# One level of Strassen for the third batch's second feed-forward product, on one Trainium2 core

## The chip, the core and the metric

The kernel runs on one core of a Trainium2 chip. The metric is the device time of one execution in microseconds (us). TensorE is PE below, VectorE DVE, ScalarE ACT, GpSimd POOL, and SyncE, which issues most of the transfers, SP. Every engine works through its own queue in order and waits on semaphores for the others.

## What is computed

For four batches of 768 rows, a retention layer (8 heads of 64) is followed by a Fourier mixing block and a feed-forward pair. The recurrence over time is done in chunks of 128 rows in the kernel; only the second half matters for this change:

```python
# attn_out: (4, 8, 768, 64) -> x: (4, 768, 512)
X = np.fft.fft(np.fft.fft(x, axis=1), axis=2)
u = x + np.real(X)
un = (u - mean(u)) / np.sqrt(var(u) + 1e-06)
ch = np.maximum(un @ w_ch1, 0.0) @ w_ch2     # 512 -> 2048 -> 512
out = u + ch
```

Inputs and output are float32; the matmuls run on float16 with float32 sums.

## The kernel before, in words

The four batches are pipelined: while the feed-forward of batch b runs, the attention of batch b + 1 is computed beside it (casts on POOL, transposes as transfers on SP, mask products and chunk states on DVE, scaled outputs on ACT), then its mixing. Each piece of work is a unit with a due time in units of batches; `emit` (L1387) sorts all units by it, and the tile framework arranges the instructions of each engine in a fixed queue. `held` (L150) ties a unit's instructions to the order in which they were written; units that are not held may be moved by the framework's scheduler.

The mixing of a row block kb (128 rows) is `s2_unit` (L993): four small matmuls into `pq`, two ACT copies, two DVE steps into u (L1019, L1022), two POOL additions. `norm_unit` (L1046) follows: statistics on DVE, then the normalised block on ACT; `unT_unit` (L1071) transposes it, for batches 2 and 3 by a transfer.

The feed-forward of batches 1 and 2 goes in two row tiles of 384. `h_unit` (L1087) computes 128 hidden features: four matmuls of 384 columns, then a ReLU on ACT or DVE by the list ACT_ROWS (L62) into ht16. `ch_unit` (L1124) computes the second product of a 128-row block: 16 matmuls of 512 columns into one PSUM tile, one DVE instruction that scales and adds u (L1135), and one transfer out.

The last batch does the second product by one level of Strassen, in Winograd's form, for three groups of 256 rows. The hidden features are split into two halves and the output columns into two halves, so that rows, features and columns make two-by-two blocks. `hp_unit` (L1169) computes hidden features n and n + 8 for 256 rows (eight matmuls of 256 columns) and does their ReLUs on ACT, the last one half on DVE. `hidden_sums` (L1193) forms four sums of hidden blocks on DVE, at the points that SUMS (L59) lists. `wsum_unit` (L1156) forms four sums of blocks of w_ch2 on DVE, in eight instructions, into buffers of the load pool `inp`. `p_unit` (L1205) computes one of the seven products: eight matmuls of 256 columns, then DVE instructions (L1235) that scale the PSUM tile and add it to u or to the output tile. Products 1, 6 and 7 accumulate in one PSUM tile which DVE reads after each of them. The order is 1, 4, 5, 6, 2, 7, 3. The PSUM pool `ps_pm` has three tiles, shared by the first and the second product.

Loads of q, k and v (`load_unit`, L189) go through the pool `inp` of 11 buffers, 12 loads to a batch, issued in SP's queue among the transposes and the outputs. Due times: TS1 and LD1 for attention and loads, DM1 and LAST_MIX for the mixing of row blocks 3 to 5, WS for the weight sums.

Of the kernel before, what the change touches and what calls it, by code (L numbers as in the profile page):

```python
# [12 lines left out]
ALU = mybir.AluOpType  # L13
f32 = mybir.dt.float32
f16 = mybir.dt.float16
# [50 lines left out]
def kernel(  # L66
# [17 lines left out]
    inp = pool("inp", 11)  # L84
# [100 lines left out]
    in_of, a_of = {}, {}  # L185
    w_dma = []
    srcs = {"q": q, "k": k, "v": v}

    def load_unit(b, i, after=None, names="qkv"):  # L189
        def run():  # L190
            h0 = 2 * PAIR_ORDER[i]
            for name in names:
# [3 lines left out]
                t = inp.tile([P, 2, NCH, D], f32, tag="in32", name=f"{name}32")  # L196
# [17 lines left out]
    def first_load(name, i, eng):  # L214
        def run():
            h0 = 2 * ORD0[i]
            t = in_of[name, 0, i] = inp.tile([P, 2, NCH, D], f32, tag="in32", name=f"{name}32")
# [869 lines left out]
    def h_unit(b, rt, fb):  # L1087
        def run():
# [6 lines left out]
            if fb in ACT_ROWS[rt]:  # L1095
# [46 lines left out]

    def flat(t):
        return t.rearrange("p h c d -> p (h c d)").bitcast(f16)

    def spare(n, name):
        return flat(inp.tile([P, 2, NCH, D], f32, tag="in32", name=name))[:, 0:n]
# [3 lines left out]
    sg = htf[:, 8 * DM:12 * DM].rearrange("p (s n k) -> p s n k", s=2, n=8)  # L1151

# [3 lines left out]
    def wsum_unit(k, part):  # L1156


        def run():
            n0, n1 = 4 * part, 4 * part + 4  # L1160
            t = seven["t", k, part] = spare(4 * 256, "wsum").rearrange("p (n m) -> p n m", n=4)
            a, b = {1: ((0, 1), (0, 0)), 2: ((1, 1), None), 3: ((1, 1), (0, 1)),
                    4: ((1, 0), None)}[k]
            in1 = half_of(w216, *b, n0, n1) if b else seven["t", k // 2, part]
            nc.vector.tensor_tensor(out=t, in0=half_of(w216, *a, n0, n1), in1=in1,
# [3 lines left out]
    def hp_unit(b, g, n):  # L1169

        def run():
            unT = lb[b]["unT"]
            if (g, n) == (0, 0):
                seven["s4"] = spare(8 * P, "s4").rearrange("p (n k) -> p n k", n=8)
# [18 lines left out]
    def hidden_sums(g, n, which):  # L1193

        sl = slice(max((0,) + tuple(m + 1 for m in SUMS[g == 2] if m < n)), n + 1)
        a11, a12 = hg[:, sl, 0, 0:P], hg[:, sl, 1, 0:P]
        a21, a22 = hg[:, sl, 0, P:256], hg[:, sl, 1, P:256]
        s1, s2, s4 = sg[:, 0, sl], sg[:, 1, sl], seven["s4"][:, sl]
        ops = ((s1, a21, a22, ALU.add), (s2, s1, a11, ALU.subtract),
# [5 lines left out]
    def p_unit(b, g, k):  # L1205


        def run():
# [6 lines left out]
            if k in (1, 2, 4):  # L1215
                seven[name] = ps_pm.tile([P, 2, 256], f32, tag="pm", name="ps7")
# [272 lines left out]
```

## Time and profile before

| | us |
|---|---|
| median of 3 runs | 241.77 (240.67 to 242.31) |
| the profiled execution | 240.73 |
| its span, first to last instruction | 238.7 |
| PE busy in the span | 225.4 |
| DVE busy | 187.4 |
| ACT busy | 125.3 |
| POOL busy | 81.4 |

The granted TensorE clock is full throughout. In the rows of a profile, "x" is the number of instructions, shapes are partitions by elements, "out<-in" are the program's names, and L is the line in the kernel. A timeline row has the start, the time from the first start to the last end of instructions merged into it, and in brackets how long the engine had been idle before it and what ended that. Busy time includes overlap of neighbours of under 0.1 us. In the chain of waits each row is a start, a length and the work that held up the rest.

### The profile page before, as it was taken

What the parts mean: (1) busy time and instruction counts of PE and PEld (TensorE: products, weight loads), DVE (VectorE), ACT (ScalarE), POOL (GpSimd) and SP (SyncE); (2) the same over time, 40 slices, a digit from 0 to 9 for tenths busy, and PEclk for the clock granted to TensorE, in tenths of its full rate; (3) what the DMA queues carried; (4) which work ended last, traced back from release to release, by engine and by line L of the source; (5) the groups of instructions that cost most, each with busy time, mean ns of one, the idle gap of its engine ahead of it and who ended that gap; (6) DMA issues with size and microseconds to landing.
All of it is one profiled execution on the core that took longest, in us unless ns stands there. A gap on an engine that the chain in (4) does not pass through costs nothing.

```text
span 238.7 us, 5575 instructions
## 1 busy us (share of the span) xinstructions
PE 225.4 (94%) x2135; PEld 155.3 (65%) x2135; DVE 187.4 (79%) x460; ACT 125.3 (52%) x273; POOL 81.4 (34%) x148
## 2 busy tenths in 40 slices
PE   0788999999999999999999999999999999999993
PEld 0356779756775646765567446655666468888893
DVE  8789887958898889986886829977895885867473
ACT  5989759674865444840247415822257326072430
POOL 8378802665300097850000826940002410220000
PEclk9999999999999999999999999999999999999999
DMA  7999999999999489979999577696100261031202
GB/s 179 233 270 239 237 206 207 210 251 248 241 235 208 72 191 221 203 138 132 249 279 218 116 161 203 130 138 156 53 3 0 45 154 25 3 110 23 91 0 91
DMA packets 100954, 36.80 MB, mean 154 GB/s; under 512 B 91456, under 2 KB 97984, under 8 KB 100928
## 3 DMA queue, kind: packets, MB, share of 16 engines
q1 hardware_dynamic: 96704, 32.25, 64.2%
q0 software_dynamic: 4224, 4.19, 10.6%
q8 instruction: 17, 0.28, 0.5%
q14 instruction: 9, 0.07, 0.1%
HBM read 27.26 MB, written 6.29 MB: 141 GB/s over the span
## 4 chain that ended last, share of the span: by engine, by line
PE 82%; DVE 6%; DMA 5%; ACT 2%; issue 1%; POOL 1%; SPq 0%; DVEq 0%; ACTq 0%
PE psc L1131 23%; PE psh L1092 21%; PE psh L1179 9%; PE ps L1231 5%; PE psh L1109 3%; PE wkA L667 3%; DMA qTz<-q16z 3%; PE ps L850 3%; DMA k<-in_k_dram 2%; PE wkY L721 2%; PE pq L1012 2%; PE ps L830 1%; DVE atm L539 1%; PE wkY L717 1%; PE wkK L686 1%
## 5 line engine op out<-in xcount | busy, mean ns | idle before, releaser
L1131 PE MATMUL psc<-w,ht 128*128 128x512 f16 x288 | 67.7, 379 | 0.0
L1092 PE MATMUL psh<-unT,w 128*128 128x384 f16 x320 | 59.5, 326 | 0.0
L1040 POOL TENSOR_TENSOR u<-u,x 128x256 f32<-128x256 f32 x21 | 13.3, 635 | 117.1 <-DVE u L1019 104.8
L1131 PEld LDWEIGHTS <-ht 128*128 128x128 f16 x288 | 27.3, 98 | 26.5
L1092 PEld LDWEIGHTS <-w 128*128 128x128 f16 x320 | 29.9, 98 | 15.9 <-DMA unT<-un 0.4
L1096 ACT ACTIVATE ht<-psh 128x384 f16<-128x384 f32 x46 | 22.3, 489 | 23.7 <-PE psh L1092 23.2
L670 DVE TENSOR_TENSOR atm<-wkA,maskp 128x512 f16<-128x512 f32 x36 | 23.6, 680 | 1.7 <-PE wkA L667 1.7
L1184 ACT ACTIVATE ht<-psh 128x512 f16<-128x512 f32 (+1 forms) x24 | 13.7, 571 | 15.6 <-PE psh L1179 11.0
L1179 PE MATMUL psh<-unT,w 128*128 128x256 f16 x192 | 21.6, 273 | 0.0
L1098 DVE TENSOR_SCALAR ht<-psh 128x384 f16<-128x384 f32 x34 | 18.7, 549 | 2.7 <-PE psh L1092 2.5
L1056 ACT ACTIVATE un<-u,stats 128x512 f16<-128x512 f32 x21 | 14.8, 717 | 10.7 <-DVE stats L1052 7.6
L1179 PEld LDWEIGHTS <-w 128*128 128x128 f16 x192 | 18.7, 98 | 2.1
L1135 DVE SCALAR_TENSOR_TENSOR ob<-psc,stats,u 128x512 f32<-128x512 f32 x18 | 13.4, 743 | 8.5 <-PE psc L1131 8.3
L696 DVE SCALAR_TENSOR_TENSOR s<-s,gk,wkK 128x128 f16<-128x128 f16 x48 | 16.1, 336 | 2.4 <-ACT s L692 1.6
L729 ACT ACTIVATE x<-wkY,gexp 128x384 f16<-128x384 f32 x24 | 12.9, 580 | 9.0 <-PE wkY L721 8.9
L1051 DVE BATCH_NORM_STATS2 bst<-u 128x6 f32<-128x512 f32 x21 | 14.4, 686 | 4.0 <-POOL u L1042 3.8
L1231 PEld LDWEIGHTS <-ht 128*128 128x128 f16 x152 | 14.1, 98 | 2.3 <-issue 0.6
L441 POOL TENSOR_SCALAR kd<-k,gexp 128x384 f16<-128x384 f32 x24 | 13.8, 585 | 3.3 <-DMA k<-in_k_dram 3.3
L667 PE MATMUL wkA<-qTz,kT 128*128 128x256 f16 x72 | 13.2, 273 | 0.3 <-DMA qTz<-q16z 0.3
L1042 POOL TENSOR_TENSOR u<-u,x 128x256 f32<-128x256 f32 x21 | 13.3, 635 | 0.0
L1014 ACT COPY qn<-pq 128x128 f32<-128x128 f32 x18 | 4.9, 274 | 15.0 <-PE pq L1012 15.0
L1203 DVE TENSOR_TENSOR ht<-ht 128x512 f16<-128x512 f16 (+2 forms) x21 | 8.1, 385 | 5.9 <-ACT ht L1184 5.6
(194 smaller groups left out, 400.9 us busy)
## 6 DMA issues: line engine op xcount, KB each, us to landing
q<-in_q_dram SPq DMA_DIRECT2D x16, 384.0 KB, 6.0
k<-in_k_dram SPq DMA_DIRECT2D x16, 384.0 KB, 5.6
v<-in_v_dram SPq DMA_DIRECT2D x16, 384.0 KB, 5.7
out_dram<-ob SPq DMA_DIRECT2D x23, 256.0 KB, 2.4
w<-in_moe_w_ch_dram POOLq DMA_DIRECT2D x8, 512.0 KB, 10.9
unT<-un SPq DMA_TRANSPOSE x15, 2.5
kT<-kd SPq DMA_TRANSPOSE x10, 3.0
qTz<-q16z SPq DMA_TRANSPOSE x8, 3.8
```

The costliest lines, as they stand in the source:

```text
L441: kc = nc.gpsimd.tensor_scalar(out=kd[:, :, h2, :], in0=k32[:, h2], scalar1=gkd[:, h0 + h2:h0 + h2 + 1], scalar2=1.0, op0=ALU.mult, op1=AL ...
L667: mm = nc.tensor.matmul(wk[:, c2], st["kT"][:, c, :], st["qT"][:, :, c, :], start=True, stop=True)
L670: nc.vector.tensor_tensor(out=st["atm"][:, 2 * part:2 * part + 2], in0=wk, in1=maskp[:, PAIR_ORDER[i]].unsqueeze(1).to_broadcast([P, 2, 2, ...
L696: nc.vector.scalar_tensor_tensor(out=s16[:, c], in0=s16[:, c - 1], scalar=gk2[:, hp:hp + 1], in1=wk[:, c - c0], op0=ALU.mult, op1=ALU.add)
L1051: nc.vector.bn_stats(bst, u[:, kb, :])
L1056: nc.scalar.activation(un, u[:, kb, :], AF.Identity, bias=stats[:, kb, 0:1], scale=-1.0)
L1092: nc.tensor.matmul(psh, w116[:, cb, fb * P:(fb + 1) * P], unT[:, cb, rt * 384:(rt + 1) * 384], start=(cb == 0), stop=(cb == 3))
L1096: nc.scalar.activation(ht16[:, fb, :], psh, AF.Relu, bias=0.0, scale=-1.0)
L1098: nc.vector.tensor_scalar(out=ht16[:, fb, :], in0=psh, scalar1=-1.0, scalar2=0.0, op0=ALU.mult, op1=ALU.max)
L1131: nc.tensor.matmul(psc, ht16[:, fb, rb3 * P:(rb3 + 1) * P], w216[:, fb, :], start=(fb == 0), stop=(fb == NFB - 1))
L1179: nc.tensor.matmul(psh[:, t], w116[:, cb, fb * P:(fb + 1) * P], unT[:, cb, g * 256:(g + 1) * 256], start=(cb == 0), stop=(cb == 3))
L1231: nc.tensor.matmul(dst, lhsT, rhs[:, c0:c1], start=bool(new and n == 0), stop=(n == 7), skip_group_check=True)
```

## The change

Batch 2, the third, takes the same form as batch 3: three groups of `hp_unit`, the seven products, and no `ch_unit`. In numbers, 128 first-product matmuls of 384 columns and 96 second-product matmuls of 512 become 192 and 168 matmuls of 256. Its units are not held; those of batch 3 are. Further:

- The weight sums are made once, due at 1.65 to 1.95 instead of 2.88 to 2.98, so beside the second batch. They stay until the end: three of the four in `wide`, four load buffers taken out of the pool (11 becomes 7), one in cd16 and sd16, tables that are no longer needed then. Until then loads use `wide` in their turn; the last batch's loads use the seven buffers alone.
- In the second batch (b = 1) all ReLUs but those of every fourth feature block go to ACT; before, ACT had 8 of 16 and 10 of 16.
- The hidden sums become three in the first half of the features and two at the end of the second, then one over all features after product 2, in place in a block that product 2 has read, and a last one after product 1. The order of the products becomes 2, 1, 4, 6, 5, 7, 3 in both batches; the scheduler is free to move those of batch 2. Product 4 shares a PSUM tile with 2 (it gets the other half), and 5 with 3. DVE adds 4 to u and to the output tile in two instructions of 256, 5 by itself.
- Due times: attention beside the third batch is stretched (TS7, 0.69 instead of 0.585), the mixing of its row blocks 3 to 5 has times of its own (MIX7), and loads are due one by one (LD1, LD2).

The core of the diff:

```diff
-LD0, LD1 = (0.223, 0.312), (-0.370, 0.140)
+TS7 = (-0.040, -0.020, 0.048, 0.69)
+LD0, LD1, LD2 = (0.223, 0.312), (-0.2425, -0.115, 0.0125, 0.14), (-0.2425, -0.115, 0.0125, 0.25)
-WS = (-0.12, -0.02)
+WS = (-0.35, -0.05)
-SUMS = ((3, 7), (2, 5, 7))
+MIX7 = {3: (0.01, 0.08, 0.10, 0.20), 4: (0.30, 0.38, 0.40, 0.45), 5: (0.42, 0.50, 0.52, 0.57)}
+SEVEN = 2
...
-    inp = pool("inp", 11)
+    inp = pool("inp", 7)
...
+    wide = const.tile([P, 4, 2, NCH, D], f32, tag="wide")
+    loads = [0]
+
+    def in_tile(name, b):
+        n = loads[0] % 11
+        loads[0] += 1
+        if b < B - 1 and n >= 7:
+            return wide[:, n - 7]
+        return inp.tile([P, 2, NCH, D], f32, tag="in32", name=f"{name}32")
...
-            if fb in ACT_ROWS[rt]:
+            if fb in ACT_ROWS[rt] or b + 1 == SEVEN and fb % 4:
...
+    def t_of(k, part):
+        if k == 1:
+            return (cd16, sd16)[part].rearrange("p a b -> p (a b)").rearrange(
+                "p (n m) -> p n m", n=4)
+        return tw[:, k - 2, 4 * part:4 * part + 4]
...
-            if n in SUMS[g == 2]:
-                hidden_sums(g, n, (0, 1) if n == 7 else (0, 1, 2, 3))
+            if n == 3:
+                hidden_sums(0, 4, (1, 2, 3))
+            elif n == 7:
+                hidden_sums(4, 8, (1, 2))
...
+        ops = {1: (s1, a21, a22, ALU.add), 2: (s2, s1, a11, ALU.subtract),
+               3: (a21, a11, a21, ALU.subtract), 4: (a12, a12, s2, ALU.subtract)}
...
-            name, half = {1: ("a", 0), 6: ("a", 0), 7: ("a", 0), 2: ("b", 0), 4: ("dc", 0),
-                          5: ("dc", 1), 3: ("dc", 1)}[k]
+            name, half, new = {2: ("bd", 0, 1), 1: ("a", 0, 1), 4: ("bd", 1, 0), 6: ("a", 0, 0),
+                               5: ("c", 0, 1), 7: ("a", 0, 0), 3: ("c", 0, 0)}[k]
...
-            if k == 1:
+            if k == 2:
+                hidden_sums(0, 8, (4,))
+            elif k == 1:
                 add(left, ps, ri, left)
-                hidden_sums(g, 7, (2, 3))
-            elif k == 2:
+                hidden_sums(4, 8, (3,))
+            elif k == 4:
                 ob = seven["ob"] = obp.tile([P, DM], f32, tag="ob", name="ob")
-                add(ob[:, 0:256], ps, ri, left)
+                add(ob[:, 0:256], seven["bd"][:, 0], ri, left)
+                add(u[:, j, 0:256], ps, rj, u[:, j, 0:256])
...
-        if b == B - 1:
+        if b >= SEVEN:
+            pinned = held if b == B - 1 else lambda unit: unit
             for g in range(3):
-                majors += [held(hp_unit(b, g, n)) for n in range(8)]
-                majors.append(held(rstd_unit(b, g, 2)))
-                majors += [held(p_unit(b, g, k)) for k in (1, 4, 5, 6, 2, 7, 3)]
+                majors += [pinned(hp_unit(b, g, n)) for n in range(8)]
+                majors.append(pinned(rstd_unit(b, g, 2)))
+                majors += [pinned(p_unit(b, g, k)) for k in (2, 1, 4, 6, 5, 7, 3)]
```

More of the change, by code (lines that the diff above doesn't have):

```diff
@@ L1251, in run @@
                 add(right, ps, ri, right)
-            elif k == 5 and tail:
-                flat_dc = seven["dc"].rearrange("p t m -> p (t m)")
-                add(u[:, j, 0:384], flat_dc[:, 0:384], rj, u[:, j, 0:384])
-                add(u[:, j, 384:DM], seven["e"], rj, u[:, j, 384:DM])
             elif k == 5:
-                add(pair(u[:, j]), seven["dc"], rj, pair(u[:, j]))
+                for dst, c0, c1 in outs:
+                    uj = u[:, j, 256 + c0:256 + c1]
+                    add(uj, dst, rj, uj)
             elif k == 7:
```

72 lines of the change are left out of this document (34 added, 38 removed).

## The prediction

> **What bounds the kernel now.** I read the busy shares first, then the busy time by stage, then the chain of work that ended last, then the timelines of PE and DVE where products are evicted.
>
> ```profile
> PE 225.4 (94%) x2135; PEld 155.3 (65%) x2135; DVE 187.4 (79%) x460; ACT 125.3 (52%) x273; POOL 81.4 (34%) x148
> ```
> ```profile
> core 0: us, PE busy (x) PEld busy (x) DVE busy (x) ACT busy (x) POOL busy (x), PEclk, DMA share, GB/s
> 142.40:168.00 25.60, 25.60 (x226) 16.05 (x226) 22.24 (x52) 11.17 (x28) 12.31 (x21) 1.00 0.74 157
> 168.00:194.40 26.40, 26.40 (x196) 15.94 (x195) 22.17 (x51) 11.23 (x25) 3.64 (x6) 1.00 0.19 43
> ```
>
> The two windows are the third batch (b = 2). PE is busy for all 52.0 us of it, so PE sets its length. But DVE is busy for 44.4 us, 85%: only 7.6 us of cover are left there. ACT has 29.6 us free.
>
> ```profile
> 170.06 0.22 PE wkA L667 x2
> 170.28 0.65 PE psh L1092 x4
> 170.93 0.29 PE wkY L717 x10
> 171.22 0.42 PE wkY L721 x12
> 171.64 5.94 PE psh L1092 x36
> ...
> 183.80 10.36 PE psc L1131 x48
> 194.16 0.23 PE pq L1012 x4
> 194.40 7.00 PE psh L1179 x64
> ...
> 215.53 6.23 PE ps L1231 x56
> ```
>
> These rows of the chain price PE's work: 0.165 us for a 384-column matmul of the first product, 0.216 for a 512-column one of the second, 0.109 for the paired first product, 0.111 for a 256-column matmul of the seven products (0.89 for a product of eight). Note that the 48 matmuls at 183.80 ran without any gap: each block has its own PSUM tile and needs DVE once in 3.5 us. The seven products are different. Products 1, 6 and 7 gather in one tile, so 6 cannot start before DVE has read 1, nor 7 before DVE has read 1+6. The last batch shows what that costs:
>
> ```profile
> 206.40 1.03 PE L1231 MATMUL ps<-wsum,ht 128*128 128x256 f16 x8 [0.42 <-DVE u L1235]
> ```
> ```profile
> 201.84 0.43 DVE L1187 TENSOR_SCALAR ht<-psh 128x256 f16<-128x256 f32 x1 [1.60 <-ACT ht L1184]
> 202.29 0.89 DVE L1203 TENSOR_TENSOR ht<-ht 128x512 f16<-128x512 f16 x2
> 203.10 0.16 DVE L1068 RECIPROCAL stats<-stats 128x2 f32<-128x2 f32 x1
> 203.36 0.48 DVE L1235 SCALAR_TENSOR_TENSOR u<-ps,stats,u 128x256 f32<-128x256 f32 x1
> 203.76 0.41 DVE L1203 TENSOR_TENSOR s<-ht 128x512 f16<-128x512 f16 x1
> 204.10 0.42 DVE L1203 TENSOR_TENSOR ht<-ht 128x512 f16<-128x512 f16 x1
> 204.43 0.74 DVE L1235 SCALAR_TENSOR_TENSOR u<-ps,stats,u 128x512 f32<-128x512 f32 x1
> 205.09 0.47 DVE L1019 SCALAR_TENSOR_TENSOR u<-pq,g,qn 128x256 f32<-128x256 f32 x1
> 205.48 0.47 DVE L1022 SCALAR_TENSOR_TENSOR u<-pq,g,qn 128x256 f32<-128x256 f32 x1
> 205.88 0.47 DVE L1235 SCALAR_TENSOR_TENSOR u<-ps,stats,u 128x256 f32<-128x256 f32 x1
> ```
>
> Product 6's eviction starts at 205.88 and ends at 206.35; product 7 starts on PE at 206.40. Ahead of it stood only sums, four evictions and two mixing steps: in the last batch DVE has little else to do. In the third it also carries the attention of the last batch.
>
> For the prices of that other work, from start to start where instructions follow without a gap:
>
> ```profile
> 151.12 0.68 DVE L1051 BATCH_NORM_STATS2 bst<-u 128x6 f32<-128x512 f32 x1
> 151.72 0.67 DVE L670 TENSOR_TENSOR atm<-wkA,maskp 128x512 f16<-128x512 f32 x1
> 152.31 0.17 DVE L1052 BATCH_NORM_AGGREGATE stats<-bst 128x2 f32<-128x6 f32 x1
> 152.40 0.66 DVE L1051 BATCH_NORM_STATS2 bst<-u 128x6 f32<-128x512 f32 x1
> 152.98 0.33 DVE L696 SCALAR_TENSOR_TENSOR s<-s,gk,wkK 128x128 f16<-128x128 f16 x1
> 153.22 0.17 DVE L1052 BATCH_NORM_AGGREGATE stats<-bst 128x2 f32<-128x6 f32 x1
> ...
> 172.33 0.56 DVE L1098 TENSOR_SCALAR ht<-psh 128x384 f16<-128x384 f32 x1 [0.69 <-PE psh L1092]
> 172.81 1.01 DVE L746 TENSOR_TENSOR xab<-x 128x768 f16<-128x768 f16 x2
> 173.74 0.55 DVE L1098 TENSOR_SCALAR ht<-psh 128x384 f16<-128x384 f32 x1
> ...
> 189.68 0.69 DVE L1165 TENSOR_TENSOR wsum<-w,wsum 128x1024 f16<-128x1024 f16 x1
> ```
>
> So: statistics 0.60, aggregate 0.09, mask product 0.59, state step 0.24, a 384-wide ReLU 0.48, two folds 0.93. From the fence above: half a mixing step 0.39, a 256-wide eviction 0.40, a 512-wide one 0.66, a 512-element hidden sum 0.34 to 0.46 (the latter if it waits for the one before it; 0.40 taken where either may be). Instructions start some 0.07 us before the one ahead ends, so the half ReLU (0.43 long) counts 0.36 and a 1024-element sum (0.69) 0.62.
>
> **The change, part by part.**
>
> *PE in the third batch.* 96 second-product matmuls (96 x 0.216 = 20.7) become 168 of 256 columns (168 x 0.111 = 18.7); the first product goes from 128 x 0.165 = 21.1 to 192 x 0.109 = 21.0. All else on PE stays. Gain 2.1 us (1.9 to 2.3), and only if PE is never kept waiting.
>
> *DVE in the third batch.* Out go 14 ReLUs (0.48 each), 6 wide evictions (0.66) and the 8 weight sums (0.62): 15.7 us. In come, for each of three row pairs, six 512-element sums, one of 1024, half a ReLU, six 256-wide evictions and one of 512: 6 x 0.40 + 0.62 + 0.36 + 6 x 0.40 + 0.66 = 6.4, or 19.3 us. Net +3.6 us: 44.4 + 3.6 = 48.0 of the 49.9 that PE would need. 96% on average, with work that comes in bursts, means stalls; the order in which the changed program's instructions stand in DVE's queue says where.
>
> The windows show PE at 100% of this stage and DVE at 85%. The Trainium skill (Perfetto Trace Analysis, Identifying the Most-Contended Engine) says to find the engine with the highest occupancy and to relieve that one first. By that rule the relief of PE counts whole and the result would be the first rival's below; the windows agree that PE is the fullest, but by the sum above the fullest engine changes with the edit.
>
> *Third pair of rows (the last products of the batch).* Let X be the end of the pair's first product. On DVE, in order, up to product 6's eviction: mixing block 0 (0.79), half ReLU (0.36), half of block 1 (0.39), sum (0.40), other half (0.39), sum (0.40), statistics 0 (0.60), the 1024 sum (0.62), aggregate (0.09), eviction 1 (0.40), sum (0.35), mixing block 2 (0.79), two statistics (1.20), aggregate, an eviction of 4, aggregate, the other of 4 (0.09 + 0.40 + 0.09 + 0.40), eviction 6 to its end (0.47): 8.2 us. PE would be ready for product 7 at X + 0.23 + 2 x 0.89 + 0.23 + 3 x 0.89 = 4.9. PE waits 3.3 us, 3.8 if the statistics of block 2 also wait for POOL, whose two additions to it (0.64 us each by the row below) start only behind that block's mixing. I take 3.6; the low end, 2.5, is for a queue that starts a little ahead.
>
> ```profile
> 185.04 0.64 POOL L1040 TENSOR_TENSOR u<-u,x 128x256 f32<-128x256 f32 x1 [1.19 <-DVE u L1019]
> ```
>
> Before, these mixing steps and statistics lay under 10.4 us of gap-free second product; that cover is gone. The last batch's first product stands behind product 3 on PE, and the transpose of block 1, whose normalising waits for the same aggregate, comes in at about the same time.
>
> *Second pair.* From its X, DVE has up to eviction 6: statistics, aggregate, four state steps, half ReLU, two sums, two folds, the 1024 sum, two folds, eviction 1, a sum, two mask products, two evictions, eviction 6: 0.60 + 0.09 + 0.96 + 0.36 + 0.80 + 0.93 + 0.62 + 0.93 + 0.40 + 0.35 + 1.18 + 0.80 + 0.47 = 8.5. PE reaches product 7 after outputs, products 2 and 1, masks, 4, masks, 5 and 6, outputs, and the next pair's first ReLU tile: 0.71 + 1.78 + 0.22 + 0.89 + 0.44 + 1.78 + 0.43 + 1.0 = 7.25. That is 1.25 us; the next pair's third ReLU tile then waits for product 3's tile, which DVE reads behind two folds, up to 0.9 more. I take 2.0 (1.2 to 2.4).
>
> *First pair.* DVE has room; product 6 waits for eviction 1 by 0.25 to 1.1, the upper end if the normalising that stands between this pair's ReLUs on ACT holds them. I take 0.7.
>
> *Last batch.* Its products now go 2, 1, 4, 6, 5, 7, 3 and its fourth sum is one 1024-element step ahead of eviction 1, which slips from 203.36 to about 204.05; then a sum, two evictions instead of one wide, the mixing: eviction 6 ends at 206.85 instead of 206.35, +0.5. In the other two pairs eviction 1 ends 3.3 us behind the first product and product 6 is ready at 2.7: +0.6 to 0.7 each, where before there was no wait. Sum 0.4 (sums at their shortest) to 1.9; I take 1.5.
>
> *Second batch and loads.* 9 ReLUs (9 x 0.48) move from DVE to ACT, which the page shows half idle, and 8 weight sums (8 x 0.62) come onto DVE: 0.7 us net there, beside gap-free matmuls. I count 0 (-0.2 to +0.5). Loads of the last batch have 7 buffers instead of 11: the last head pair's loads wait for the first pair's casts, and its own casts stand on POOL behind a mixing step that DVE reaches some 8 us after the first X. The mask products that need them stand on PE some 20 us after it (the rest of the products, the next first product, two products more). Casts, of the length of POOL's 0.64, and transposes fit between. Cost 0; if they did not fit, the matmuls would wait one for one.
>
> Sum: -2.1 + 0.7 + 2.0 + 3.6 + 1.5 = +5.7. The profiled execution took 240.73 us, 2.0 of it around its span of 238.7, which the change does not touch; so 246.4. The median of the runs, 241.77, is 1.0 above the profiled one; I keep the profiled base and let the top of the range take that 1.0.
>
> **The rivals.**
> - *DVE keeps up.* PE's 2.1 us arrive whole: 238.6; with the 0.42 wait at 206.40 gone too, 238.2. It decides if eviction 6 of the third pair ends within 4.9 us of X, so if 3.3 us of the queue ahead of it lie earlier. For it: DVE's ACT-fed sums leave it idle while a first product runs. Against it: the mixing steps ahead of eviction 6 need matmuls that PE makes only just before. 11%.
> - *Half of the stalls.* DVE, ahead by one to two us at each pair, leaves 2 to 4 us of stalls in all: 240.5 to 242.5, about as before. 20%.
> - *Loads come late.* SP's queue holds outputs, transposes and loads in one line; if the last pair's loads sit behind an output that waits for a late eviction, 1 to 4 us come on top of my sum: 247.5 to 250.5. For it: 7 buffers; against it: the 20 us above. 5%.
> - *My sum*, with the stalls between their bounds: -2.3 + 0.25 + 1.2 + 2.5 + 0.4 = +2.0 at the least, 242.8, up to 249.2 below. 64%.
>
> **How the numbers follow.** One per cent (2.4 us) is about what a measurement of this kernel can tell from no change. Even the full gain of 2.1 lies within it, so faster by more has 6%: the first rival with the wait and a little of ACT's relief. Same: the rest of the first and the second, 25%. Slower: 69%. The range reaches from 240.0, so that it takes in the second rival and leaves out the first, to 249.2: -1.9 + 1.1 + 2.4 + 3.9 + 1.9 + 0.1 = +7.5, and the 1.0 of the median. The likeliest case alone has 242.8 to 249.2.
>
> **What would show it.** In the profile after: PE waits on DVE evictions at product 6 or 7 in the third batch, longest in its third pair (3 us or more together), with DVE near full from the second pair on; the last batch's first product starting 3 to 5 us later than 194.40 and not 2 earlier; short waits before product 6 in the last batch. I am wrong if DVE shows idle time inside the products of the third batch, or if the last batch starts near 192.

## The result, and the profile after

The changed kernel takes 249.28 us (median of 4 runs, 248.26 to 250.47) against 242.04 for the kernel before, run beside it: 1.031 times, 95% interval 1.0245 to 1.0377. It is slower, as forecast, but by more than forecast, and 0.08 us above the top of the range. Five more runs on another chip gave 1.0366 (1.0328 to 1.0404). Four executions of the kernels below took over 1.5% longer than the fastest of their kernel, one of them, of the changed kernel, 591.07 us: they stand in the medians and ranges, but not in the ratios and counts. The profiled execution took 248.76 us, its span 246.7, so 8.0 more than before.

The first view is the page's busy shares, the second the busy time by stage, the two windows of the third batch. In a window row stand its length, then busy time and number of instructions of PE, PEld, DVE, ACT and POOL, then the granted clock.

```profile
PE 226.0 (92%) x2271; PEld 168.3 (68%) x2271; DVE 192.8 (78%) x473; ACT 133.3 (54%) x289; POOL 83.9 (34%) x148
```
```profile
142.63:168.00 25.37, 24.48 (x266) 21.75 (x265) 20.39 (x49) 12.80 (x30) 12.43 (x20) 1.00 1.01 208
168.00:198.80 30.80, 26.38 (x286) 22.89 (x285) 27.66 (x72) 13.78 (x30) 4.65 (x7) 1.00 0.13 36
```

DVE's 48.06 us is the forecast's 48.0. PE, which was busy for all of its 52.0 us, now stands still for 5.3 of 56.2, and DVE is at 90% in the second window. The waits of PE from the second batch on say on what (total, times, longest):

```profile
PE ps L1245 <- DVE u L1249: 4.3, 4, 3.0
PE ps L1245 <- DVE ht L1199: 1.6, 5, 0.8
PE psh L1191 <- DMA unT<-un: 1.6, 1, 1.6
PE psh L1191 <- DVE u L1249: 0.3, 1, 0.3
```

The longest wait stands in the third pair of rows. PE's timeline there, then DVE's:

```profile
193.02 1.03 PE L1245 MATMUL ps<-wide,ht 128*128 128x256 f16 x8 [0.27 <-DVE u L1249]
197.08 1.03 PE L1245 MATMUL ps<-wide,ht 128*128 128x256 f16 x8 [3.03 <-DVE u L1249]
197.95 1.04 PE L1245 MATMUL ps<-w,ht 128*128 128x256 f16 x8
198.82 0.39 PE L1024 MATMUL pq<-gk,g16r 128*128 128x129 f16 x4
200.82 2.36 PE L1191 MATMUL psh<-unT,w 128*128 128x256 f16 x20 [1.60 <-DMA unT<-un]
```
```profile
188.46 0.48 DVE L1031 SCALAR_TENSOR_TENSOR u<-pq,g,qn 128x256 f32<-128x256 f32 x1 [1.01 <-ACT qn L1027]
...
195.04 0.69 DVE L1063 BATCH_NORM_STATS2 bst<-u 128x6 f32<-128x512 f32 x1 [0.35 <-POOL u L1054]
195.65 0.17 DVE L1064 BATCH_NORM_AGGREGATE stats<-bst 128x2 f32<-128x6 f32 x1
195.73 0.45 DVE L1249 SCALAR_TENSOR_TENSOR ob<-ps,stats,u 128x256 f32<-128x256 f32 x1
196.10 0.17 DVE L1064 BATCH_NORM_AGGREGATE stats<-bst 128x2 f32<-128x6 f32 x1
196.19 1.24 DVE L1249 SCALAR_TENSOR_TENSOR u<-ps,stats,u 128x256 f32<-128x256 f32 x3
```

The three instructions at 196.19 are the second of product 4, the sixth eviction (to 197.03) and product 5's; product 7 starts at 197.08. Ahead of it DVE has worked for 8.6 us with one gap of 0.35, as forecast (8.2 to 8.7). What was not forecast is the last row of PE: the last batch's first product waits 1.6 us more, for the transposes of block 1.

By start times on PE: the third batch's first product or mixing step begins 0.29 us later than before (142.63 against 142.34), the last batch 6.59 (200.82 against 194.23), and PE's last product starts 8.08 later (242.36 against 234.28).

### The profile page after: what moved, and what is told of

It reads as the page before. It is cut to its first block, busy times and chain, and to the rows that moved or that the text cites. A ratio compares the mean times of both kernels' runs of the same rounds, so it can differ in the third digit from the quotient of the medians.

```text
span 246.7 us, 5881 instructions
## 1 busy us (share of the span) xinstructions
PE 226.0 (92%) x2271; PEld 168.3 (68%) x2271; DVE 192.8 (78%) x473; ACT 133.3 (54%) x289; POOL 83.9 (34%) x148
## 5 line engine op out<-in xcount | busy, mean ns | idle before, releaser
L1191 PE MATMUL psh<-unT,w 128*128 128x256 f16 x384 | 45.3, 272 | 2.0 <-DMA unT<-un 1.6
L1143 PE MATMUL psc<-w,ht 128*128 128x512 f16 x192 | 45.3, 379 | 0.0
L1191 PEld LDWEIGHTS <-w 128*128 128x128 f16 x384 | 37.1, 98 | 6.6 <-DMA unT<-un 1.8
L1196 ACT ACTIVATE ht<-psh 128x512 f16<-128x512 f32 (+1 forms) x48 | 27.1, 571 | 26.1 <-PE psh L1191 19.1
L1245 PEld LDWEIGHTS <-ht 128*128 128x128 f16 x352 | 32.3, 98 | 12.3 <-issue 5.6
L1104 PE MATMUL psh<-unT,w 128*128 128x384 f16 x192 | 35.8, 326 | 0.1
L1143 PEld LDWEIGHTS <-ht 128*128 128x128 f16 x192 | 18.1, 98 | 17.4
L1217 DVE TENSOR_TENSOR ht<-ht 128x512 f16<-128x512 f16 (+1 forms) x42 | 19.6, 478 | 8.1 <-ACT ht L1196 7.7
L1108 ACT ACTIVATE ht<-psh 128x384 f16<-128x384 f32 x37 | 17.9, 489 | 12.2 <-PE psh L1104 11.3
L1104 PEld LDWEIGHTS <-w 128*128 128x128 f16 x192 | 17.9, 98 | 9.5 <-issue 0.4
L1245 PE MATMUL ps<-wide,ht 128*128 128x256 f16 x144 | 18.8, 272 | 4.4 <-DVE u L1249 4.3
L1245 PE MATMUL ps<-w,ht 128*128 128x256 f16 (+1 forms) x144 | 18.5, 270 | 1.7 <-DVE ht L1199 1.6
```

What stands on the lines that cost most here:

```text
L1104: nc.tensor.matmul(psh, w116[:, cb, fb * P:(fb + 1) * P], unT[:, cb, rt * 384:(rt + 1) * 384], start=(cb == 0), stop=(cb == 3))
L1108: nc.scalar.activation(ht16[:, fb, :], psh, AF.Relu, bias=0.0, scale=-1.0)
L1143: nc.tensor.matmul(psc, ht16[:, fb, rb3 * P:(rb3 + 1) * P], w216[:, fb, :], start=(fb == 0), stop=(fb == NFB - 1))
L1191: nc.tensor.matmul(psh[:, t], w116[:, cb, fb * P:(fb + 1) * P], unT[:, cb, g * 256:(g + 1) * 256], start=(cb == 0), stop=(cb == 3))
L1196: nc.scalar.activation(hg[:, n, t0:t1], psh[:, t0:t1], AF.Relu, bias=0.0, scale=-1.0)
L1217: nc.vector.tensor_tensor(out=out_, in0=x, in1=y, op=op)
```

## The experiments

Theory A, after the comparison: DVE's queue sets the end of each pair of the third batch, and the last batch's new order costs 1.5 us. Rivals: the loads with fewer buffers, the SP queue, slower matmuls. Ratios are to the kernel before on the same chip, with the 95% interval. Times in a bracket are the runs' range.

**Everything but the third batch's Strassen.**

```diff
-SEVEN = 2
+SEVEN = 3
```

> Everything of the change except the third batch's Strassen step: that batch has its old row-block products and ReLUs again; the new order and sums of the last batch, the 7 load buffers, and the rest stay. Only the limit SEVEN goes from 2 to 3, so the ReLUs given to ScalarE and the weight sums both come one batch later than in the changed kernel. Theory A (the third batch's VectorE queue makes the loss): only the last batch's new order costs, 1.5 us, so about 242.3 in a profiled run (before 240.7), the last batch's first product starting at about 194 to 195 us, the third batch without waits on VectorE. Rival B (fewer load buffers, the SP queue and the loads behind it make most of it): the third batch is still long, last batch from 198 us or later, time above 246.

Measured: 244.52 us (243.3 to 245.55), 1.0129 (1.0097 to 1.0162). Both theories missed. In the profiled execution, the slowest of the six, the last batch began at 197.45, so 3.2 later than before; 1.5 of it is one row, and it does wait for a load's transposing transfer:

```profile
163.53 0.39 PE L679 MATMUL wkA<-qTz,kT 128*128 128x256 f16 x2 [1.49 <-DMA kT<-kd]
```

The change delays the last loads and stretches the attention with them; this kernel had the late loads and the old attention. So the stretch was put back in:

```diff
-                t1 = TS1 if b < SEVEN else TS7
+                t1 = TS1 if b < B - 2 else TS7
```

> The run without the third batch's Strassen step (e_rest), but with the last batch's attention spread over the third batch as the changed kernel spreads it (TS7 instead of TS1). In e_rest a mask product waited 1.5 us for the last loads, which the change issues later, while the attention still came at its old time. Theory A1 (the late loads cost only where the attention is not stretched with them, as the change does): the wait of 1.5 us for kT is gone, last batch's first product at 195.5 to 196.5 instead of 197.4, about 243.0. Rival B1 (7 buffers keep the loads late in any case): the wait stays or grows, 244.5.

Measured: 244.22 us (244.13 to 244.25), 1.0133 (1.0099 to 1.0167). The wait for kT is gone and the last batch begins at 196.32, as A1 has it, but it still waits, because the stretched attention ends too late for the blocks' transposes, and the median is close to e_rest's and not A1's 243.0:

```profile
196.32 7.15 PE L1191 MATMUL psh<-unT,w 128*128 128x256 f16 x64 [1.37 <-DMA unT<-un]
```

So the late loads, or the attention stretched to make room for them, have a price of 1.4 to 1.5 us in one place or the other. In the changed kernel no mask product waits for kT, and where the long wait is filled (below) the last batch does not wait for its transposes either. That DVE's stalls cover the price there is argued, not shown.

**The last batch's old order.** Its products and sums in the form of before; the third batch as changed.

```diff
-                majors += [pinned(p_unit(b, g, k)) for k in (2, 1, 4, 6, 5, 7, 3)]
+                majors += [held(p_old(b, g, k)) for k in (1, 4, 5, 6, 2, 7, 3)] if b == B - 1 else \
+                    [pinned(p_unit(b, g, k)) for k in (2, 1, 4, 6, 5, 7, 3)]
```

> The changed kernel with the last batch's three pairs in the form of before: products in the order 1, 4, 5, 6, 2, 7, 3, the hidden sums of before, one wide eviction of the pair 4 and 5. The third batch as changed. Theory A: the last batch's products cost 1.5 us by their new order, and nothing else moves: from the last batch's first product (200.8 us) to PE's end 40.7 us instead of 42.2; in all about 247.3. Rival: the last batch was lengthened by what the third batch leaves behind (late outputs and loads on SP's queue), not by its own order: 42.2 stays.

Measured: 247.34 us (246.73 to 247.81), 1.0252 (1.022 to 1.0283). Theory A: from the first product's start to the last one's it takes 40.07 us (200.29 to 240.36), with the new order 41.54 (200.82 to 242.36).

**Two ways to shorten the third pair.** First the mixing of block 2 goes into the last batch:

```diff
-LAST_MIX = {3: (0.0, 0.07, 0.09, 0.20), ...
+LAST_MIX = {2: (0.0, 0.05, 0.07, 0.12), 3: (0.06, 0.12, 0.14, 0.20), ...
...
-            streams += mix_units(b + 1, [0, 1, 2], *(end + t for t in da[2:]))
+            streams += mix_units(b + 1, [0, 1, 2] if b < SEVEN else [0, 1], *(end + t for t in da[2:]))
```

> The changed kernel, but the mixing, normalising and transpose of the last batch's block 2 move from ahead of the third pair's products into the last batch. Theory A: of VectorE's 8.2 to 8.7 us ahead of the third pair's sixth eviction two half mixing steps (0.8) and the statistics and aggregate (0.7) go, so the waits in the third pair's products fall from 3.9 to about 2.4, and the wait of the last batch's first product for the transposes of block 1 from 1.8 to 0 to 1. Last batch from 198.0 to 199.0 us instead of 200.8; in all 245 to 247 instead of 248.8, if the moved block finds room in the last batch. Rival B (the transposes are late because of the SP queue's own order or the DMA, not of VectorE): the third pair gets shorter, but the wait for the transposes grows by as much, and the last batch still begins at 200.5 or later.

Measured: 250.24 us (248.46 to 252.51), 1.0359 (1.0319 to 1.04): no gain. The wait at product 7 fell only to 2.6, since block 1's statistics still stand ahead of the sixth eviction; the last batch began at 199.49 instead of 200.82, but its first products then waited 0.7 for ReLUs (0.22 and 0.45, where the changed kernel has 0.17). The granted clock was 0.50 from 195 to 198, which no theory had. Second, the evictions of products 1 and 6 are left out:

```diff
-                add(left, ps, ri, left)
+                if b != SEVEN:
+                    add(left, ps, ri, left)
```

> The changed kernel without the evictions of products 1 and 6 in the third batch (their addition to the result is left out, so the third batch's output is incomplete; the products themselves are all made). Theory A (product 6 and 7 wait because their shared accumulator must be read): the waits of 0.2 to 3.0 us at products 6 and 7 of the third batch vanish, 4.3 us of PE's waits in it; in the third pair the transposes of block 1 then become the limit, which hang on VectorE's statistics and not on the evictions, so the last batch's first product starts only 0.8 to 2.5 us sooner (198.3 to 200.0), and the whole is 246 to 248. Rival C (PE itself is slower in the 256-column products than counted): the third batch keeps its length within 0.5 us.

Measured: 247.68 us (245.65 to 249.9), 1.024 (1.0194 to 1.0285). The waits at products 6 and 7 go, so they are those of the shared accumulator, and the last batch begins at 198.20; C falls. But product 3 then waits 2.19 for DVE: the queue is what is late. Again the clock fell behind the wait.

**The sums on another engine.**

```diff
-            nc.vector.tensor_tensor(out=out_, in0=x, in1=y, op=op)
+            (nc.vector if b == B - 1 else nc.gpsimd).tensor_tensor(out=out_, in0=x, in1=y, op=op)
```

> The changed kernel with the third batch's sums of hidden blocks on GpSimd, which is busy 4.7 of 30.8 us in that batch's second half, instead of VectorE. Theory A (VectorE's queue is the bound): 1.8 us go from the queue ahead of the third pair's sixth eviction, 9 us from the batch; waits of the second pair 1.6 to about 0.5, of the third 3.7 to about 2, the transposes earlier by as much; the last batch begins at 197.5 to 199, the whole 245.0 to 247.0. Rival D (GpSimd takes long enough over them that products 5, 6 and 3 wait for GpSimd instead, 0.64 us for 256 elements against VectorE's 0.40): no gain, 248.5 to 251.

Measured: 263.87 us (262.61 to 265.48), 1.0935 (1.0898 to 1.0972): D, and worse than it had. The same 512-element sum takes 1.16 us on POOL and 0.42 on DVE:

```profile
L1217 POOL TENSOR_TENSOR ht<-ht x21: 1151/1157/2427, 148.1 to 209.0; 128x512 f16<-128x512 f16 x18, 128x1024 f16<-128x1024 f16 x3
L1217 DVE TENSOR_TENSOR ht<-ht x21: 416/424/693, 222.0 to 256.0; 128x512 f16<-128x512 f16 x18, 128x1024 f16<-128x1024 f16 x3
```

The mixing's additions then stand behind the sums on POOL, DVE's statistics wait for them (8.9 us), and the evictions behind these: PE waits 10.2 us for evictions and 4.0 for the sums. The clock has a part in it: it stood at 0.50 for three stretches of 6.8 us behind these waits. With the half ReLU on ACT and the last batch's old order besides:

> The changed kernel with three mends together: the third batch's hidden sums on GpSimd, its half ReLU on ScalarE, and the last batch's products and sums in the form of before. Theory A: the gains of the parts add up, 1.0 for the half ReLU, 2.5 to 4 for the sums, 1.5 to 1.9 for the last batch: 242.5 to 244.5, and PE's gain of 2.1 us is still not enough to pass the kernel before (241.0). Rival G (something else bounds the third batch as soon as VectorE is relieved, ScalarE or GpSimd): 245 or more.

Measured: 262.03 us (260.08 to 264.59), 1.0848 (1.0798 to 1.0897), with waits of 4.7 and 5.7 us for evictions.

**Fewer sums.** This leaves DVE's queue shorter and nothing else changed:

```diff
-            elif n == 7:
+            elif n == 7 and (b, g) != (SEVEN, 2):
                 hidden_sums(4, 8, (1, 2))
...
-                hidden_sums(0, 8, (4,))
+                if (b, g) != (SEVEN, 2):
+                    hidden_sums(0, 8, (4,))
```

(and the sum after product 1 likewise.)

> The changed kernel without the four hidden sums behind the first product of the third batch's third pair (old sums are used, so two blocks of the third batch's output are not the reference's); 0.40 + 0.40 + 0.62 + 0.35 = 1.8 us less on VectorE ahead of the sixth eviction, nothing else changed. Theory A (VectorE's queue sets the end of the pair): product 7 starts 1.4 to 1.8 us sooner than in the changed kernel (197.08 us there), at 195.3 to 195.7; the wait before it is 1.2 to 1.6, too short for the clock to fall or the transposes to be late; the last batch begins at 197.1 to 197.6 against 198.9 with the wait filled, and the whole is 244.9 to 245.6. Rival I (the mixing's chain through PE and ScalarE sets it, and VectorE would wait for that): less than 0.7 us sooner, 246 or more.

Measured: 247.14 us (246.7 to 247.8), 1.0242 (1.0181 to 1.0303). PE's rows:

```profile
195.28 1.03 PE L1245 MATMUL ps<-wide,ht 128*128 128x256 f16 x8 [1.81 <-DVE u L1249]
...
199.15 7.16 PE L1191 MATMUL psh<-unT,w 128*128 128x256 f16 x64 [1.73 <-DMA unT<-un]
```

Product 7 starts 1.80 us sooner for 1.8 us less on DVE: one for one, theory A. But the last batch began at 199.15 and not at A's 197.1 to 197.6, and the time missed A's 244.9 to 245.6, because the transposes were late again, though A took the wait for too short for that.

**The long wait filled.** Product 5 of the third pair is computed 4, 2, 3 and 6 times; the repeats stand where PE waits:

```diff
-            for dst, c0, c1 in outs:
+            for dst, c0, c1 in outs * (4 if (b, g, k) == (SEVEN, 2, 5) else 1):
```

> The changed kernel with product 5 of the third batch's third pair computed four times over instead of once (same tile, started anew each time, so the result stays), 2.7 us of matmuls that stand in the place where PE waits 3.0 us for VectorE. In three of the runs so far the granted clock stood at 0.50 for some 3 us behind that wait. Theory E (the long wait lets PE's clock fall): no half clock there, mean clock back to 0.998 or more in all runs, and 0.7 to 1.5 us less in the median: 247.8 to 248.6. Rival F (the clock falls for another reason, or it costs nothing because VectorE or the transposes set the end anyway): the same as the changed kernel, 249.3, or up to 0.5 more from the later eviction of product 5.

> The changed kernel with product 5 of the third pair computed twice (one repeat, 0.89 us), so that about 2.1 us of the 3.0 us wait are left. Theory E (the clock falls behind a long wait, and the transposes land late with it): a clock stretch at 0.50 followed waits of 2.2 and 2.6 us in two other runs, so it still comes in some executions: 248 to 250, mean clock below 0.997 in some, transposes landing in 3 us or more in the profile. If one repeat already does it: 247.0 and a clock of 0.998 or more in all. Rival F (no link with the wait): 249.3 to 250.3, as the changed kernel.

> Product 5 computed three times (two repeats, 1.8 us), about 1.2 us of the wait left. Theory E: clock 0.998 or more in every run, transposes landing in about 2.4 us, 247.0 as with three repeats. Rival F: 249.3 to 250.3, transposes in 3.9 to 4.1 us.

> Product 5 computed six times (five repeats, 4.45 us, 1.4 us more than the wait). Theory E: the clock stays up, but product 7 starts 1.2 to 1.6 us later than in e_warm and all behind it too: 248.2 to 248.8. If repeated matmuls themselves brought the gain (a busier PE and not a shorter wait), more of them would not cost: 247.0 or less.

Measured: three repeats 247.05 us, 1.0273 (1.0225 to 1.0321); one repeat 246.77, 1.0295 (1.0241 to 1.0349); two 246.96, 1.0275 (1.0258 to 1.0293); five 247.87, 1.0315 (1.0297 to 1.0334). More work on PE and, by the ratios to the changed kernel beside it, 1.7 to 2.2 us less time, up to where the wait is full; five repeats take 0.9 more than two, so the gain is not the matmuls'. With one repeat the clock still fell in one execution of four (248.9 us), as E had it, but block 1's transposes already landed in 2.4. The changed kernel beside it:

> The changed kernel once more, on the chip of the mended ones, to size the gains against it: 1.031 times the kernel before by every theory, its granted clock below 0.997 in most runs if theory E (the 3.0 us wait lets PE's clock fall) is right, with a stretch of some 3 us at 0.50 behind the third pair's long wait in a profile that has it.

Measured: 1.0366 (1.0328 to 1.0404), most runs from 249.9 to 250.9. Its profile has the fallen clock. Windows (PEclk is the third number from the right):

```profile
195.00:196.00 1.00, 0.00 (x0) 0.00 (x0) 0.79 (x3) 0.00 (x0) 0.18 (x1) 1.00 0.40 87
196.00:197.00 1.00, 0.00 (x0) 0.00 (x0) 1.00 (x4) 0.93 (x2) 0.00 (x0) 0.55 0.00 0
197.00:200.00 3.00, 2.74 (x14) 1.95 (x14) 1.34 (x3) 0.40 (x1) 0.00 (x0) 0.50 0.50 90
...
203.00:204.00 1.00, 1.00 (x11) 0.90 (x10) 0.36 (x1) 0.68 (x2) 0.61 (x2) 1.00 0.03 10
```

The clock goes to 0.50 while PE stands still and stays there for 7 us; the last batch's first 64 matmuls take 8.07 us where 7.15 is full speed. Each execution lists its mean clock, and by that the fall goes with PE's longest wait from the second batch on, as each kernel's profile has it:

| wait, us | kernels | executions with a mean clock below 0.995 |
|---|---|---|
| 5.5 to 5.7 | e_pool, e_best | 11 of 11 |
| 3.0 | changed, e_lastold, e_shift | 14 of 18 |
| 2.2 to 2.6 | e_later, e_nogate, e_fill1 | 6 of 12 |
| 1.8 or less | the ten others | 1 of 45 |
| 0.4 | before, beside these runs | 1 of 61 |

The one in 45 is the profiled execution of the kernel with three repeats (250.4 us): its clock stands at 0.95 throughout, with no stretch at 0.50, so this is another loss. The one of the kernel before (243.69 us, 0.993) has no profile. A mean clock alone does not tell one loss from the other. A stretch at 0.50 behind the long wait stands in the second profile of the changed kernel and in those of e_lastold, e_later, e_nogate, e_pool and e_best; in the first profile of the changed kernel and those of e_shift and e_fill1 the clock stayed up behind waits of 2.3 to 3.0.

The Trainium skill (TensorE: Matmul & The Clock Gate, What's actually happening) says that the array's clock is halved after an idle window of about 3.4 us, and that the window runs freely. The traces agree on the half, and executions of one kernel that differ go with a window that runs freely; but here 2.2 us of standing still could bring it (e_nogate), less than the window it names, while the stretches at 0.50 lasted 3.4 us or twice that.

**The late transposes.** In the changed kernel and in e_nosum the transfer of block 1 landed after 4.1 and 4.3 us, in the kernels with a filled wait after 2.4. The wait's length is not the reason (1.8 in e_nosum, 2.3 in e_fill1). In each profile the slow transfers were those in flight when the queue that feeds instructions (q8) moved its packet. The table has the first of them; in the changed kernel, e_lastold and e_nosum block 2's was in flight too and took 3.0 to 4.0:

| kernel | q8 packet in the half us from | slow transfer: issued, landed after | block 1 landed after |
|---|---|---|---|
| changed | 198.5 | block 1, 196.6, 4.1 | 4.1 |
| e_lastold | 198.0 | block 1, 196.3, 4.0 | 4.0 |
| e_nosum | 196.5 | block 1, 194.8, 4.3 | 4.3 |
| e_fill1 | 193.5 | block 0, 193.2, 3.6 | 2.4 |
| e_mend | 192.5 | block 0, 192.1, 3.3 | 2.4 |

In all 20 profiles, from 185 us on, the 90 transposes with no packet of q8 between their issue and their landing took 2.3 to 2.5 us. Of the 30 with one, 28 took 3.0 to 4.5. One of these is in the kernel before (3.6, issued at 189.1), where nothing waited for it.

The queue, in the transfers' view of the changed kernel from 198 to 199 us (packets, MB, share of the 16 engines):

```profile
q1 hardware_dynamic: 426, 0.10, 51.5%
q8 instruction: 1, 0.02, 5.8%
```

Over the span it moved 17 packets and 0.28 MB, so 16 KB each; PE's 2 x 2271 instructions, over 17, are about 267 to a packet, which speaks for PE's program. The Trainium skill (Runtime: NRT & Kernel Launch, Instruction fetch mechanics) has blocks of 16 KiB or 256 instructions, fetched over a DMA queue of the sequencer's own at a cost that is mostly hidden; the trace agrees on the size, not on the cost. If the fetch is the cause, a few instructions more ahead of the wait must move it, also without filling the wait:

```diff
-            for dst, c0, c1 in outs:
+            for dst, c0, c1 in outs * (2 if (b, g, k) == (SEVEN, 1, 5) else 1):
```

> The changed kernel with product 5 computed twice in the second pair of the third batch instead of the third pair: eight matmuls and eight weight loads more, 0.87 us of PE's time, 18 us ahead of the long wait, which stays unfilled. VectorE's order is the same. Theory J (the transposes of block 1 are slow because PE's fetch of its next 16 KB of instructions falls on them, released by the same evictions that end PE's wait): the fetch now comes before the wait, at 193 to 195.5 us, the transposes of block 1 land in 2.3 to 2.6, the last batch's first product does not wait for them by more than 0.3, and starts 1 to 2 us sooner than in the changed kernel (200.8), in spite of 0.87 us more on PE; the wait ahead of product 7 stays at 2.2 to 3.1, so the clock still falls in some executions: 246.8 to 249. Rival K (they are slow because PE has stood still): landing in 3.9 to 4.1 again, a wait of 1.6 for them, the last batch from 200.8 or later, 249 or more.

Measured: 249.21 us (247.49 to 249.65), 1.0342 (1.0312 to 1.0372). The packet came at 194.5; the transfers' row (block 0 slow, the others not) and PE's:

```profile
DMA to landing us min/median/max: 2.4/2.5/3.2
```
```profile
197.55 1.03 PE L1245 MATMUL ps<-wide,ht 128*128 128x256 f16 x8 [3.03 <-DVE u L1249]
198.42 1.04 PE L1245 MATMUL ps<-w,ht 128*128 128x256 f16 x8
199.29 0.39 PE L1024 MATMUL pq<-gk,g16r 128*128 128x129 f16 x4
199.62 4.65 PE L1191 MATMUL psh<-unT,w 128*128 128x256 f16 x41
```

Theory J, by the rows: the wait of 3.03 is the same to the hundredth, the last batch begins 1.2 us sooner with 0.87 us more on PE, and waits for no transfer. By the time alone K could not be told from it (249.21, where J had up to 249), because the clock fell in four of the five executions. This kernel also prices the clock: 247.49 in the execution at 1.0, 249.16 to 249.65 in the four at 0.990 to 0.993.

**The place of the mixing, and the mends together.** The attention is made to end earlier, with three repeats of product 5 and then without:

```diff
-TS7 = (-0.040, -0.020, 0.048, 0.69)
+TS7 = (-0.040, -0.020, 0.048, 0.62)
```

> The changed kernel with product 5 four times over (clock kept up) and the last batch's attention spread over 0.62 of the third batch instead of 0.69, so that its mixing comes earlier: out of the queue ahead of the third pair's sixth eviction, into the second pair. Theory A (VectorE's sum of work in the batch bounds it, not its place): what the third pair gains the second loses, 246.5 to 247.5 (e_warm: 247.05). Rival H (only the place matters, the third pair's queue and the late transposes): the waits of the third pair and of the transposes go, 3 to 4 us, and the second pair loses 1 at most: 243.5 to 245.

> The changed kernel with the last batch's attention spread over 0.62 of the third batch instead of 0.69, and nothing repeated. In e_ts the sixth eviction of the third pair ended at 197.3 us, while PE with its repeats came to product 7 at 199.27, without them at 196.6. Theory A (VectorE's sum of work in the batch bounds it): a wait of about 0.7 at product 7, product 7 at 197.3, the last batch from 199.0 to 199.6 us, where the filled kernels have 198.9; no wait long enough for the clock to fall; 246.8 to 247.6 in all. Rival H (the place of the mixing matters, and with it moved the batch gets shorter than in the filled kernels): last batch before 198.3, 246.0 or less.

Measured: 249.37 us, 1.0343 (1.0309 to 1.0377), inconclusive, since the repeats stood in no wait; without them 248.16, 1.0299 (1.0264 to 1.0334). Transposes in 2.4, clock 1.0 in all, the wait at product 7 down to 0.98, and still the last batch began at 200.41 (0.4 of it from a later start of the third), later than by either theory, and the time missed A's 246.8 to 247.6 as well: at product 2's end PE now waited 0.84 for ACT's ReLU and 0.52 for the half ReLU, which stood behind the mixing on DVE. H falls; DVE's work cost something in each place that was tried.

The repeats, the half ReLU on ACT (`n == 7 and b == B - 1`), and the last batch's old order; then block 2's mixing moved as well:

> The changed kernel with product 5 of the third pair four times over (the clock stays up), the third batch's half ReLU on ScalarE, and the last batch's products and sums in the form of before; the sums of the third batch on VectorE as changed. If the three parts add (theory A with E): 2.2 for the clock, 0.8 to 1.0 for the half ReLU, 1.5 for the last batch, from 249.3: 244.6 to 245.0. If the half ReLU only moves the wait on (the sums that follow it then wait for ScalarE): 245.6.

> As the run before it (e_mend), and the mixing of the last batch's block 2 moved into the last batch as in e_later. In e_later the clock fell behind a wait of 2.6 us and hid what the move gave; with the clock kept up, theory A expects the last batch to begin 1.0 to 1.5 us sooner than in e_mend, and 243.5 to 244.2 in all. If the block only costs in the last batch what it frees in the third: the same as e_mend.

Measured: 244.06 us (244.0 to 244.44), 1.0123 (1.009 to 1.0157); and 245.73, 1.0197 (1.0163 to 1.0232). The parts add, slightly better than forecast. The wait at product 2's end is gone, and one of 0.38 at product 6 stands in its place. Moving block 2 gives back more than it gains, against both forecasts for it: the last batch waits 1.07 for transposes and 0.67 for a ReLU. PE's rows of the better one, with the repeats up to 195.5:

```profile
195.70 1.03 PE L1333 MATMUL ps<-wide,ht 128*128 128x256 f16 x8 [0.19 <-DVE u L1337]
...
197.76 1.48 PE L1192 MATMUL psh<-unT,w 128*128 128x256 f16 x12
```

The third batch still takes 55.4 us (142.38 to 197.76) against 51.9 before. No version beats the kernel before.

## Why the prediction was right in kind and short in size

- **PE's gain of 2.1, DVE's 3.6 more.** DVE's sum was right (48.06 against 48.0). A product of eight takes 0.87 from start to start where it isn't held up (0.89 counted). C fell with e_nogate. The rule that the forecast quotes from the Trainium skill (Perfetto Trace Analysis, Identifying the Most-Contended Engine) says of TensorE that its headroom is to be judged by its FLOPs or by the share of its weight loads. The weight loads filled 62% of this stage before (15.94 and 16.05 of 52.0 us), less than DVE's 85%, so the rule read whole did not single out PE.
- **Third pair, 3.6.** Right: 3.3 in the rows' waits, 3.9 against products that run on without a gap. Of the difference, 0.3 is lost at product 2, where the last matmul waits for the half ReLU, and 0.3 in starting again (a product takes 1.03 from a standstill). e_nosum shows the mechanism one for one.
- **Second pair, 2.0.** Measured 1.0 in the rows' waits and 1.5 from start to start, but elsewhere: product 7, for which 1.25 was counted, did not wait. Product 2 waited for the half ReLU, product 6 for eviction 1, and the next pair's first product for a tile.
- **First pair, 0.7.** The size was near (0.96) by luck, the place wrong: not product 6 waited, but the last matmul of product 2, for the half ReLU, which stood behind three mask products on DVE. e_mend takes that wait away.
- **Last batch, 1.5.** The size was right, 1.5, and e_lastold gives it back, so the new order and its sums are the cause; the place was wrong here too. About 1.2 of it, from start to start, is lost at the end of product 2 in the three pairs, again for the half ReLU. Product 6's wait of 0.39 replaces the 0.42 that product 7 had before.

The rows of PE for these: first and second pair of the third batch, then the last batch.

```profile
153.15 1.05 PE L1245 MATMUL ps<-w,ht 128*128 128x256 f16 x8 [0.81 <-DVE ht L1199]
170.90 1.16 PE L1245 MATMUL ps<-w,ht 128*128 128x256 f16 x9 [0.16 <-DVE ht L1199]
175.02 1.03 PE L1245 MATMUL ps<-wide,ht 128*128 128x256 f16 x8 [0.56 <-DVE u L1249]
176.74 0.81 PE L1191 MATMUL psh<-unT,w 128*128 128x256 f16 x6 [0.28 <-DVE u L1249]
...
208.91 1.16 PE L1245 MATMUL ps<-w,ht 128*128 128x256 f16 x9 [0.17 <-DVE ht L1199]
213.31 1.03 PE L1245 MATMUL ps<-wide,ht 128*128 128x256 f16 x8 [0.39 <-DVE u L1249]
223.43 1.16 PE L1245 MATMUL ps<-w,ht 128*128 128x256 f16 x9 [0.23 <-DVE ht L1199]
237.17 1.16 PE L1245 MATMUL ps<-w,ht 128*128 128x256 f16 x9 [0.23 <-DVE ht L1199]
```

The order before began with product 1, which does not read what the half ReLU writes. The new one begins with product 2, whose last matmul does, and so all six pairs lose 2.8 us there together (0.96, 0.34, 0.30, 0.36, 0.42 and 0.41 from start to start). The forecast has no such term; its terms for product 6 happened to be about as large.

- **Second batch and loads, 0.** 0.3 ahead of the third batch in this execution, none in e_fill1's (142.38 against 142.34). The paragraph allows 0.5 for this, the top of the range counts 0.1. No matmul of the changed kernel waits for a load, as forecast; in e_rest and e_rest7 the late loads or the stretched attention are worth 1.4 to 1.5, and what hides that in the changed kernel was not shown.
- **Transposes of block 1, counted at 0 ("comes in at about the same time").** This is the step that failed. By PE's and DVE's times it was true: with the fetch out of the way (e_fill1, e_shift) the last batch starts within 0.1 us of when it could. In the changed kernel the transfer met PE's instruction fetch, and the start waited 1.6 us more.
- **The clock, not in the forecast.** It took PE's full speed for granted behind a wait of 3 us. e_shift has the price: 1.7 to 2.2 us, from one execution against four. Where both come together they overlap: with the clock at 0.50 PE reaches the last batch late enough not to wait for the transposes (201.05). In the profiled execution of the result the clock was full, so there, of these two, the transposes alone made the time longer.

The sum without these two is the forecast's: the kernel with one repeat took 246.69 us in its profiled execution, +6.0 on the 240.73 before, where +5.7 was forecast. The rival in which loads come late gave the right time (247.5 to 250.5) with the wrong mechanism. The rival in which DVE keeps up fell with the 5.3 us in which PE stands still, and the one with half of the stalls, which had 2 to 4 us of them, with the time.

What stays open: why a fetch that occupies one DMA engine for 0.9 us (5.8% of 16 engines in 1 us) makes a transfer 1.6 us later; what decides in an execution whether the clock falls; and how much of the 249.28 is the clock's, since in the four executions behind it the mean clock does not go with the time (248.26 at 0.993, 248.76 at 0.999, 249.8 at 0.990, 250.47 at 0.996).

## What to carry to other kernels

When the fullest engine is relieved onto one at 85% of the same stage, write down the second engine's queue, in its order, up to the instruction that frees the accumulator: that sum came out right to 0.2 us here. With a new order of products, ask of each matmul which operand comes last: product 2's cost 2.8 us that nobody had counted. Then ask what a wait of several microseconds brings besides itself: a slower clock afterwards, and transfers released by the same instruction that lets the waiting engine run on. To tell such a wait's own length from its consequences, fill it with work that changes nothing: if the time falls, it was the consequences. Such a fill also moves the instruction fetches, so it takes a second change, like e_shift, to tell the two apart.

## What the runs showed of the hardware

- Behind waits of 2.2 to 3.0 us the mean clock was below 0.995 in 20 of 30 executions, behind 1.8 or less in 1 of 45, and that one lost its clock in another way. In the profiles PE's granted clock fell to 0.50 between 1.9 us (the changed kernel's second profile) and 2.7 us (e_nogate) after PE came to a stand, and stayed there for 3.4 us in e_later, e_lastold and e_nogate, 6.8 in the changed kernel.
- A transposing transfer in flight during an instruction fetch landed in 3.0 to 4.5 us instead of 2.3 to 2.5, in 28 of 30 cases.
- A sum of two 128x512 float16 tensors takes 1.16 us on POOL and 0.42 on DVE, 2.43 and 0.69 for 1024.
